# Two single tiles become a pair, and a later pair is projected early, in a fused attention and GLU kernel

## The chip, the cores and the metric

The kernel runs on one core of a Trainium2 chip. The core has a matrix engine (TensorE, PE in the profile; its weight loads are listed as PEld), a vector engine (VectorE, DVE), a scalar engine (ScalarE, ACT), GpSimd (POOL) and SyncE (SP), which here issues the DMAs. The engines run their own instruction streams and wait for one another by semaphores. The metric is the device time of one execution in microseconds; the times shown are medians of several executions.

## The reference

The input `x` has 2048 tokens of 576 values. Two kinds of layers alternate, A B A B, with the same weights both times, each added to its input:

```python
x = x + _A_ref(_layernorm(x), A_wqkv, A_wo)
x = x + _B_ref(_layernorm(x), B_w_gate, B_w_up, B_w_down)
x = x + _A_ref(_layernorm(x), A_wqkv, A_wo)
x = x + _B_ref(_layernorm(x), B_w_gate, B_w_up, B_w_down)
```

A is a local attention with 32 heads of 18 values. It projects the input to q, k and v. A token looks at 8 positions: itself and those 2, 4, ... 14 tokens before it. A softmax over the 8 logits weights the 8 v rows, and the result goes through `wo`. B is a gated unit without a nonlinearity: `(x @ w_gate) * (x @ w_up)` with 4608 columns, then `@ w_down`. Nothing looks further back than 14 tokens, so tokens can be worked on in order, in blocks.

## The kernel before

**Tiles and stages.** 128 tokens are a tile, 16 in all, taken in two groups of eight. A group goes through the first A and B layer, then through the second. A stage is one attention (`attention`, called with its number j) and one GLU (`glu`) for one tile or for a pair of tiles. In the first group's first layer tiles 0, 1, 2 and 3 are stages of their own (j = 0 to 3), tiles 4 and 5 are the pair j = 4, tiles 6 and 7 the pair j = 5. All later stages are pairs; there are 18 stages.

**Forms on TensorE.** A single tile's matmuls use all 128 rows of the array and stream 128 columns (lines 876 and 887 gate and up, 928 and 929 down, 527 the q, k, v projection, 826 the output projection). A pair's matmuls use 64 rows each, two of them side by side, and stream 256 columns (lines 900, 968 and 969, 527, 805). A pair's GLU runs in three phases of six units; a unit is two column blocks of 128 for both gate and up. A single's GLU also has three phases, each of three units of four blocks.

**One attention.** `head` normalizes a tile: statistics on VectorE (lines 414 and 415), the reciprocal root and the scaled copy on ScalarE (429, 430, 439), then the transpose, either on TensorE with a copy by ScalarE (452, 454, 457) when `on_pe` is set, or as a DMA transpose from SP (445). The projection's results are copied out by ScalarE (611, 621, 638, 645). VectorE forms the eight products of q with shifted k (676, 697) and adds them up in part (680 to 685); TensorE sums them to logits with the matrix `Esel` (691); VectorE and ScalarE do the softmax (717 to 731). The probabilities are then spread to all values of a head: with `on_pe` by TensorE with `Bsel` into the bank `pa`, one bank at a time, each copied out by ScalarE (742, 611); otherwise through DRAM by one write and four reads on SP's queue. VectorE multiplies them with shifted v (772) and adds up (786). The output projection follows, and VectorE adds the residual (796). A second `head` prepares the GLU's input. The scratch buffers of products, partial sums and probabilities exist once, so an attention's products wait for the sums of the attention before it.

**PSUM.** The GLU, the projections of q, k and v, and the output projection of pairs share bank pairs (`unit`), three of them at first. The fourth consists of `acct`, which single GLUs use, and `pa`, which the attentions with `on_pe` use; it becomes a unit after the last attention with `on_pe`, j = 4.

**Early work.** Tiles 4 and 5 are loaded into a scratch half of the residual buffer of tiles 2 and 3 (`xtmp`) at the start, and normalized and transposed inside the attention j = 3 (rank 4 there). Their q, k and v have their own place (`q_x`, `kv_x`) in the residual buffers of tiles 4 to 7.

**Order.** Nothing is ordered by hand on the engines. Each step is recorded by `op` with its engine, an assumed cost, what it reads and writes, and a rank. `Plan.run` then places the steps one by one, when the kernel is built, into fixed queues: it takes the step that can start first by the assumed costs, and prefers a lower rank that is ready about then. An attention has its own number as rank, a GLU rank 60, the steps that empty a GLU's banks rank -1. `margin` puts a step later than its inputs are assumed to be ready; `after` binds it to another step.

The pieces that decide the points touched:

```python
        if j == 4:
            return ["x"], q_x, kv_x, 0
        z = (j + 1) % 2
...
        on_pe = j < 5
        prio, mg = (1, 0) if fast else (3, 500 if j < 6 else 1200)
...
                nst = 1 if l == 0 and t < 4 else NST
```

Of the kernel before, what the change touches and what calls it, by code (L numbers as in the profile page):

```python
# [169 lines left out]
def kernel(  # L170
# [12 lines left out]
    nc = tc.nc  # L183
# [222 lines left out]
    def head(src, keys, nst, dst, key, prio, ab, on_pe, mg, c0=0, halves=False):  # L406
# [3 lines left out]
        for i in range(nst):  # L410
            def stats(i=i):
                xr = src(i).rearrange("p (a b) -> p a b", a=2)
                for a in range(2):
                    nc.vector.bn_stats(out=st[:, ia + i, a, :], in_=xr[:, a, :])
# [8 lines left out]
            op("DVE", 970, stats, r=[keys[i]], w=[f"mv{ab}{ia + i}", f"st{ab}{ia + i}0", f"st{ab}{ia + i}1"], prio=prio)  # L423
# [4 lines left out]
        def rs():  # L428
# [3 lines left out]
        op("ACT", 440, rs, r=mk + ["eps"], w=rk, prio=prio)  # L432
        op("DVE", 75, lambda: nc.vector.scalar_tensor_tensor(nmr[:, sl], mv[:, sl, 0], -1.0, rstd[:, sl], op0=ALU.mult, op1=ALU.mult),
           r=mk + rk, w=nk, prio=prio)
        for i in range(nst):
            def apply(i=i):
                x, y = src(i), xn[ia + i]
                sc = dict(bias=nmr[:, ia + i:ia + i + 1], scale=rstd[:, ia + i:ia + i + 1])
                nc.scalar.activation(y[:, 0:D], x, ACT.Identity, **sc)
                if not on_pe:  # L440
                    nc.scalar.activation(y[:, D:D + TL], x[:, KF * P:D], ACT.Identity, **sc)
            op("ACT", 770 if on_pe else 1100, apply, r=[keys[i], nk[i], rk[i]], w=[f"xn{ab}{ia + i}"], prio=prio)
# [41 lines left out]
    def place(j, nst):  # L484
# [3 lines left out]
        if j == 4:  # L488
            return ["x"], q_x, kv_x, 0
        z = (j + 1) % 2  # L490
        return [2 * z, 2 * z + 1], qT_[z][:], kv_[z][:, :, :, 0:HALO + CH], 0

    def attention(j, la, t0, nst):
# [3 lines left out]
        on_pe = j < 5  # L497
        prio, mg = (1, 0) if fast else (3, 500 if j < 6 else 1200)
# [7 lines left out]
        if j != 4:  # L506
            head(lambda i: xin[:, i0 + i, :], xin_k, nst, xnT_A, "xA", prio, 0, on_pe, mg, c0)
# [9 lines left out]
        def project(tag, au, bu, tl, ea, eb, dkeys):  # L517
# [32 lines left out]
            if nst == 2:  # L550
                o = None
                fs = {ka: {}, kb: {}}
                for first in (True, False):
                    for u, key, parts in ((ua, ka, au), (ub, kb, bu)):
                        r0, r1 = (0, 1) if first else (1, 0)
                        kw = dict(pair=(ua, ub), margin=400) if o is None else dict(after=o, need=u)
# [30 lines left out]
            else:  # L587
# [11 lines left out]
                o1 = pieces(ua, au, ka, True, False, late["wo"] if 2 <= j < 4 else None, margin=400, pair=(ua, ub))  # L599
# [44 lines left out]
        else:  # L644
# [12 lines left out]
           r=zk("k0", "k2", "k4", "v0", "v2", "v4"), w=hk, prio=prio)  # L657
        if j == 3:
            pl.rank = 4
            head(lambda i: xtmp[:, i, :], ["xt0", "xt1"], NST, xnT_A, "xA", prio, 0, on_pe, mg)  # L660
            pl.rank = 3
# [72 lines left out]
        op("DVE", 86 + 2.05 * n, soft3, r=["Lt", "zs"], w=["s13"], prio=prio - 1)  # L734
        if on_pe:
# [56 lines left out]
        guard = {3: ["xt0", "xt1"], 5: zk_x}.get(j, [])  # L792
# [40 lines left out]
        head(lambda i: xs_f[:, i0 + i, :], fk, nst, xnT_B[j % NXB], f"xB{j % NXB}_", prio - 1, 1, on_pe, mg, halves=fast)  # L833
# [19 lines left out]
    def glu(j, t0, nst, last):  # L853
# [148 lines left out]
        for ph in range(nph):  # L1002
# [37 lines left out]
            settle(ph, use)  # L1040

    seq = []
    for g0 in range(0, NTT, GT):
        for l in range(n_al):
            t = g0
            while t < g0 + GT:
                nst = 1 if l == 0 and t < 4 else NST
                seq.append((l, t, nst))
                t += nst
# [5 lines left out]
    load_x(2, 1)  # L1055
    load_x(3, 1)
# [6 lines left out]
    for j, (l, t0, nst) in enumerate(seq):  # L1063
        if l == 0 and j >= 4:
# [5 lines left out]
        if j == 4:  # L1070
# [40 lines left out]
```

## Time and profile before

| what | value |
|---|---|
| median of 3 executions | 1057.23 us (1056.66 to 1058.14) |
| the profiled execution, its time | 1056.22 us |
| its span, first to last instruction | 1054.4 us |
| TensorE busy | 1040.7 us, 99% |
| VectorE busy | 786.2 us, 75% |
| ScalarE busy | 410.8 us, 39% |
| mean granted TensorE clock | 0.998 |

The profile is one execution. Its times count from the first instruction of the span. A row of the view by stretches gives the stretch, its length, and for each engine the busy time in it with the number of instructions in brackets; the last three numbers are the granted TensorE clock as a share of full speed, the busy share of the DMA engines, and GB/s. If the view is limited to one engine, only its column stands there, and if limited to one line of the kernel, only that line's instructions are counted. A row of the view in order of time gives start, duration, engine, line, operation, what is written and read, and in brackets the idle time of the engine before it and what ended it. Matmuls overlap their neighbours by some tenths of a microsecond, so the distance from one start to the next says more than a duration.

### The profile page before, as it was taken

The page shows a single profiled execution, that of the slowest core. Times are in us where ns is not written, and L with a number is a line of the kernel's source. Part 1 is how long each engine was busy: PE and PEld are TensorE (multiplying, and loading weights), DVE is VectorE, ACT ScalarE, POOL GpSimd, SP SyncE. Part 2 cuts the span into 40 slices and gives each one's busy share as a digit, 9 for nine tenths or more (in the row PEclk, how much of TensorE's full clock was granted, in tenths as well). Part 3 has the DMA queues.
Part 4 walks back from the last instruction along what each step waited for, and adds up shares of the span by engine and source line. Part 5 has one row for each costly group of instructions (what it writes and reads, how often), then busy time and mean ns, then how long its engine had stood idle before and what let it go on. Part 6 is the DMA issues. An engine that isn't in the chain of part 4 may idle for free.

```text
span 1054.4 us, 39972 instructions
## 1 busy us (share of the span) xinstructions
PE 1040.7 (99%) x17845; PEld 829.9 (79%) x17863; DVE 786.2 (75%) x1477; ACT 410.8 (39%) x1090; POOL 8.9 (1%) x33
## 2 busy tenths in 40 slices
PE   7999999999999999999999999999999999999998
PEld 4888878787788898778887777877887788777776
DVE  7688989786979996979798876676878758833332
ACT  6752254343334544333434323334344252232221
POOL 3000000000000000000000000000000000000000
PEclk9999999999999999999999999999999999999999
DMA  9966563524262543254444534334353334343332
GB/s 272 317 186 194 177 185 104 155 63 145 69 149 81 146 105 107 70 149 128 120 93 107 140 114 118 93 115 95 93 151 82 99 90 126 116 135 96 116 101 69
DMA packets 146828, 133.68 MB, mean 127 GB/s; under 512 B 42272, under 2 KB 146016, under 8 KB 146656
## 3 DMA queue, kind: packets, MB, share of 16 engines
q1 hardware_dynamic: 146656, 131.13, 44.1%
q8 instruction: 139, 2.28, 0.9%
q14 instruction: 33, 0.27, 0.1%
HBM read 118.51 MB, written 4.06 MB: 116 GB/s over the span
## 4 chain that ended last, share of the span: by engine, by line
PE 82%; DVE 11%; DMA 4%; SPq 1%; issue 1%; ACT 1%; DVEq 0%; ACTq 0%
PE pg L900 15%; PE pu L900 14%; PE pu L968 9%; PE pg L968 8%; PE pa L900 5%; PE acct L900 5%; PE pg L527 4%; PE pu L527 3%; PE pu L876 3%; PE pg L876 3%; PE pg L928 2%; DVE scr L772 2%; DVE oT L786 2%; DMA scr<-a_dram 2%; DVE h L912 2%; PE pg L805 1%
## 5 line engine op out<-in xcount | busy, mean ns | idle before, releaser
L900 PE MATMUL pg<-xnT_B,wg 64*128 64x256 bf16 x3072 | 395.3, 269 | 0.5 <-DVE xf L796 0.5
L900 PE MATMUL pu<-xnT_B,wu 64*128 64x256 bf16 x3072 | 395.0, 269 | 0.5
L900 PEld LDWEIGHTS <-wg 64*128 64x128 bf16 x4032 | 367.7, 94 | 29.7 <-issue 2.6
L900 PEld LDWEIGHTS <-wu 64*128 64x128 bf16 x4032 | 366.8, 94 | 23.5 <-issue 0.6
L968 PE MATMUL pg<-wd,h 64*128 64x512 bf16 (+1 forms) x972 | 252.0, 377 | 0.8 <-DVE h L912 0.8
L968 PE MATMUL pu<-wd,h 64*128 64x512 bf16 (+1 forms) x971 | 252.1, 377 | 0.0
L912 DVE TENSOR_TENSOR h<-pu,g_sb 128x512 bf16<-128x512 f32 x228 | 153.5, 686 | 73.8 <-ACT g_sb L911 69.7
L968 PEld LDWEIGHTS <-h 64*128 64x128 bf16 (+1 forms) x1992 | 115.1, 94 | 100.3 <-DVE h L912 2.9
L911 ACT CAST g_sb<-pg 128x512 bf16<-128x512 f32 x228 | 132.1, 586 | 127.6 <-PE pg L900 91.6
L471 ACT COPY tok<-pu 1x1 f32<-1x1 f32 x254 | 37.4, 147 | 258.7 <-PE pu L900 191.8
L900 PE MATMUL acct<-xnT_B,wg 64*128 64x256 bf16 x960 | 130.7, 269 | 0.0
L900 PE MATMUL pa<-xnT_B,wu 64*128 64x256 bf16 x960 | 130.6, 269 | 0.0
L969 PEld LDWEIGHTS <-h 64*128 64x128 bf16 (+1 forms) x1992 | 114.1, 95 | 1.3 <-issue 0.6
L527 PEld LDWEIGHTS <-wqkv 64*128 64x128 bf16 (+1 forms) x2044 | 103.2, 94 | 15.0 <-issue 2.6
L900 PE MATMUL pg<-xnT_B,wgu_t 64*128 64x256 bf16 x384 | 103.3, 269 | 0.0
L900 PE MATMUL pu<-xnT_B,wgu_t 64*128 64x256 bf16 x384 | 103.3, 269 | 0.0
L969 PE MATMUL pa<-wd,h 64*128 64x64 bf16 (+1 forms) x540 | 102.1, 189 | 0.1
L969 PE MATMUL acct<-wd,h 64*128 64x64 bf16 (+1 forms) x540 | 102.1, 189 | 0.0
L697 DVE TENSOR_TENSOR scr<-qT,kv 128x1280 bf16<-128x1280 bf16 x104 | 82.4, 816 | 25.9 <-ACT kv L611 25.9
L786 DVE TENSOR_TENSOR oT<-oT,scr 128x1280 bf16<-128x1280 bf16 (+1 forms) x119 | 90.9, 764 | 3.2
L527 PE MATMUL pg<-xnT_A,wqkv 64*128 64x256 bf16 (+2 forms) x826 | 92.6, 260 | 0.5 <-ACT wqkv L355 0.3
L527 PE MATMUL pu<-xnT_A,wqkv 64*128 64x256 bf16 (+2 forms) x786 | 90.1, 262 | 0.8 <-DVE kv L609 0.4
(156 smaller groups left out, 1598.2 us busy)
## 6 DMA issues: line engine op xcount, KB each, us to landing
wd<-in_B_w_down_dram SPq DMA_DIRECT2D x324, 288.0 KB, 4.4
scr<-a_dram SPq DMA_DIRECT2D x52, 128.0 KB, 2.7
wg<-in_B_w_gate_dram SPq DMA_DIRECT2D x6, 768.0 KB, 10.0
wu<-in_B_w_up_dram SPq DMA_DIRECT2D x6, 768.0 KB, 11.3
out_dram<-xf SPq DMA_DIRECT2D x16, 144.0 KB, 3.0
xb<-in_A_x_dram SPq DMA_DIRECT2D x6, 288.0 KB, 2.9
a_dram<-scr SPq DMA_DIRECT2D x13, 128.0 KB, 2.4
scr<-in_A_wqkv_dram SPq DMA_DIRECT2D x4, 288.0 KB, 3.6
```

What stands on the lines that cost most here:

```text
L471: box["at"] = nc.scalar.copy(tok[0:1, :], src())
L527: return nc.tensor.matmul(bank(p_, u)[0:m, e * n:(e + 1) * n], lhsT=wqkv[r_, k, w0:w0 + m], rhs=xnT_A[r_, k, c0:c0 + n], start=start, stop ...
L697: op("DVE", 70 + 2.6 * n, lambda p_=p_, e=e: nc.vector.tensor_tensor(late["prod"][p_ % 2][:, e, :, 0:n], qT[:, :, 0:n], kT[:, :, HALO - DI ...
L772: nc.vector.tensor_tensor(js(dst), js(vT[:, :, o0:o0 + n]), abw, op=ALU.mult)
L786: op("DVE", 70 + 2.63 * n, lambda i_=i_: nc.vector.tensor_tensor(oT[:, :, 0:n], oT[:, :, 0:n], late["prod"][i_ % 2][:, 0, :, 0:n], op=ALU. ...
L876: nc.tensor.matmul(pt[:, e * n:(e + 1) * n], lhsT=w_[:, k, ft * P:(ft + 1) * P], rhs=xT[:, k, 0:n], start=(first and k == 0 and e == 0), s ...
L900: return nc.tensor.matmul(ps[:, e * n:(e + 1) * n], lhsT=w_, rhs=xT[rows, k, 0:n], start=(first and e == 0 and k == 0), stop=(not first an ...
L911: op("ACT", 490, lambda: nc.scalar.copy(g_sb[gs][:, 0:ul], pg[use["slot"]][:, 0:ul]), r=[f"wg_{j}_{u}"], w=[f"g{gs}"], prio=0, due=True)
L912: op("DVE", 605, lambda: nc.vector.tensor_tensor(hb[hs][:, 0:ul], pu[use["slot"]][:, 0:ul], g_sb[gs][:, 0:ul], op=ALU.mult), r=[f"wu_{j}_{ ...
L928: nc.tensor.matmul((pg, pu)[i][use["slot"]][:], lhsT=lhs, rhs=wt[:, e % 2, 0:512], start=first, stop=fin)
L968: return [lambda: nc.tensor.matmul((pg, pu)[i][use["slot"]][:], lhsT=lhs, rhs=wt[rows, e % 2, 0:512], start=first, stop=fin, skip_group_ch ...
L969: lambda: nc.tensor.matmul((pg, pu)[i][tl["slot"]][:, 0:TL], lhsT=lhs, rhs=wt[rows, e % 2, 512:D], start=first, stop=fin, skip_group_check ...
```

## The change

Tiles 2 and 3 become the pair j = 2, so tiles 4 and 5 are j = 3, tiles 6 and 7 are j = 4, and there are 17 stages. Numbers that name stages move by one or two accordingly: places of q, k and v, the margins, the guards on buffers, and the release of `acct` and `pa`, now after j = 2. `on_pe` holds for j < 3, so the pair of tiles 4 and 5 now spreads its probabilities through DRAM and has its GLU input transposed by DMA; its first `head` runs in attention j = 2, on TensorE.

Tiles 6 and 7 are loaded into `xtmp` once tiles 4 and 5 have been read from it. `head` can be split into its normalizing part (`parts="n"`) and its transposing part (`parts="t"`). For tiles 6 and 7 the first part stands in attention j = 2, behind the step that writes the probabilities (`xr=["s13"]`), the second in attention j = 3. Their projection (j = 4) is bound behind the end of the GLU of stage 1 (`late["glu1"]`). That of tiles 2 and 3 stays bound behind the output projection of tile 0. The second `head` of j = 2 gets priority 0, a margin of 200 and statistics by halves.

```diff
-    def head(src, keys, nst, dst, key, prio, ab, on_pe, mg, c0=0, halves=False):
+    def head(src, keys, nst, dst, key, prio, ab, on_pe, mg, c0=0, halves=False, parts="nt", xr=()):
...
-        if j == 4:
+        if j == 3:
             return ["x"], q_x, kv_x, 0
-        z = (j + 1) % 2
+        z = 1 if j == 2 else j % 2
...
-        on_pe = j < 5
-        prio, mg = (1, 0) if fast else (3, 500 if j < 6 else 1200)
+        on_pe = j < 3
+        prio, mg = (1, 0) if fast else (3, 500 if j < 5 else 1200)
...
-        if j != 4:
+        if j not in (3, 4):
             head(lambda i: xin[:, i0 + i, :], xin_k, nst, xnT_A, "xA", prio, 0, on_pe, mg, c0)
...
-                        kw = dict(pair=(ua, ub), margin=400) if o is None else dict(after=o, need=u)
+                        kw = dict(pair=(ua, ub), margin=400, after=late.get({2: "wo", 4: "glu1"}.get(j))) if o is None else dict(after=o, need=u)
...
-                o1 = pieces(ua, au, ka, True, False, late["wo"] if 2 <= j < 4 else None, margin=400, pair=(ua, ub))
+                o1 = pieces(ua, au, ka, True, False, None, margin=400, pair=(ua, ub))
...
+        if j == 2:
+            pl.rank = 3
+            head(lambda i: xtmp[:, i, :], ["xt0", "xt1"], NST, xnT_A, "xA", prio, 0, on_pe, mg)
+            pl.rank = 4
+            load_x(6, 2, True)
+            pl.rank = 2
         if j == 3:
             pl.rank = 4
-            head(lambda i: xtmp[:, i, :], ["xt0", "xt1"], NST, xnT_A, "xA", prio, 0, on_pe, mg)
+            head(lambda i: xtmp[:, i, :], ["xt0", "xt1"], NST, xnT_A, "xA", prio, 0, False, mg, parts="t")
             pl.rank = 3
...
+        if j == 2:
+            pl.rank = 4
+            head(lambda i: xtmp[:, i, :], ["xt0", "xt1"], NST, xnT_A, "xA", prio, 0, False, mg, parts="n", xr=["s13"])
+            pl.rank = 2
...
-        guard = {3: ["xt0", "xt1"], 5: zk_x}.get(j, [])
+        guard = {2: ["xt0", "xt1"], 4: zk_x}.get(j, [])
...
-        head(lambda i: xs_f[:, i0 + i, :], fk, nst, xnT_B[j % NXB], f"xB{j % NXB}_", prio - 1, 1, on_pe, mg, halves=fast)
+        head(lambda i: xs_f[:, i0 + i, :], fk, nst, xnT_B[j % NXB], f"xB{j % NXB}_", 0 if j == 2 else prio - 1, 1, on_pe, 200 if j == 2 else mg, halves=fast or j == 2)
...
+        late[f"glu{j}"] = chain["pe"]
...
-                nst = 1 if l == 0 and t < 4 else NST
+                nst = 1 if l == 0 and t < 2 else NST
...
-    load_x(2, 1)
-    load_x(3, 1)
+    load_x(2, 2)
     load_x(4, 2, True)
...
-        if l == 0 and j >= 4:
+        if l == 0 and j >= 3:
             load_x(t0, nst)
...
-        if j == 4:
+        if j == 2:
             op("PE", 0, lambda: None, w=list(pool_keys["pa"]) + ["acct"], free="unit", use={"slot": NB})
```

More of the change, by code (lines that the diff above doesn't have):

```diff
@@ L404 @@
     wok = ["wo_z", "wot0", "wot1"] + [f"wo{dd}" for dd in range(4)]
-    def head(src, keys, nst, dst, key, prio, ab, on_pe, mg, c0=0, halves=False):
+    def head(src, keys, nst, dst, key, prio, ab, on_pe, mg, c0=0, halves=False, parts="nt", xr=()):
         mv, st, rstd, nmr, xn = mv_[ab], st_[ab], rstd_[ab], nmr_[ab], xn_[ab]
         ia = c0 // P
-        for i in range(nst):
+        for i in range(nst if "n" in parts else 0):
             def stats(i=i):
@@ L422, in head @@
                 continue
-            op("DVE", 970, stats, r=[keys[i]], w=[f"mv{ab}{ia + i}", f"st{ab}{ia + i}0", f"st{ab}{ia + i}1"], prio=prio)
+            op("DVE", 970, stats, r=[keys[i], *xr], w=[f"mv{ab}{ia + i}", f"st{ab}{ia + i}0", f"st{ab}{ia + i}1"], prio=prio)
         mk = [f"mv{ab}{ia + i}" for i in range(nst)]
@@ L431, in head @@
         rk = [f"rstd{ab}{ia + i}" for i in range(nst)]
-        op("ACT", 440, rs, r=mk + ["eps"], w=rk, prio=prio)
-        op("DVE", 75, lambda: nc.vector.scalar_tensor_tensor(nmr[:, sl], mv[:, sl, 0], -1.0, rstd[:, sl], op0=ALU.mult, op1=ALU.mult),
-           r=mk + rk, w=nk, prio=prio)
+        if "n" in parts:
+            op("ACT", 440, rs, r=mk + ["eps"], w=rk, prio=prio)
+            op("DVE", 75, lambda: nc.vector.scalar_tensor_tensor(nmr[:, sl], mv[:, sl, 0], -1.0, rstd[:, sl], op0=ALU.mult, op1=ALU.mult),
+               r=mk + rk, w=nk, prio=prio)
         for i in range(nst):
@@ L441, in apply @@
                     nc.scalar.activation(y[:, D:D + TL], x[:, KF * P:D], ACT.Identity, **sc)
-            op("ACT", 770 if on_pe else 1100, apply, r=[keys[i], nk[i], rk[i]], w=[f"xn{ab}{ia + i}"], prio=prio)
+            if "n" in parts:
+                op("ACT", 770 if on_pe else 1100, apply, r=[keys[i], nk[i], rk[i]], w=[f"xn{ab}{ia + i}"], prio=prio)
+            if "t" not in parts:
+                continue
             cs = slice(c0 + i * P, c0 + (i + 1) * P)
```

## The prediction

> **What bounds the kernel now.** I read the page's head first, then the chain of work that ended last, then the span cut at the stage borders.
>
> ```profile
> span 1054.4 us, 39972 instructions
> PE 1040.7 (99%) x17845; PEld 829.9 (79%) x17863; DVE 786.2 (75%) x1477; ACT 410.8 (39%) x1090; POOL 8.9 (1%) x33
> PE 82%; DVE 11%; DMA 4%; SPq 1%; issue 1%; ACT 1%; DVEq 0%; ACTq 0%
> ```
>
> ```profile
> 60.00:111.00 51.00, 50.74 (x776) 40.15 (x776) 42.49 (x100) 19.12 (x42) 0.00 (x0) 1.00 0.53 163
> 111.00:188.00 77.00, 76.37 (x1209) 61.62 (x1215) 69.09 (x135) 34.07 (x76) 0.00 (x0) 1.00 0.54 155
> 188.00:400.00 212.00, 210.10 (x3682) 174.41 (x3682) 180.47 (x332) 88.43 (x249) 0.00 (x0) 1.00 0.43 113
> 400.00:1054.00 654.00, 650.23 (x11427) 514.17 (x11423) 450.28 (x806) 229.68 (x645) 0.00 (x0) 1.00 0.39 109
> ```
>
> The columns are length, then busy time of PE, PE's weight loads, DVE, ACT and POOL, then granted clock, DMA share and GB/s. From 60 us on TensorE is idle for 0.26, 0.63, 1.90 and 3.77 us in the four stretches. So whatever shortens its instruction stream shortens the kernel one for one, and whatever makes it wait costs one for one. VectorE is next: 42.49 of 51 and 69.09 of 77 us while the first four GLUs run.
>
> That VectorE share decides how soon an attention is ready. Here are VectorE's stretches from the first score product of one attention to that of the next (single tile 2, single tile 3, pair 4 and 5, pair 6 and 7).
>
> ```profile
> 61.03:87.57 26.54, 22.02 (x52) 1.00 0.49 155
> 87.57:115.36 27.79, 23.70 (x56) 1.00 0.63 192
> 115.36:165.91 50.55, 45.26 (x88) 1.00 0.58 162
> 165.91:215.24 49.33, 41.56 (x75) 1.00 0.48 136
> ```
>
> The attentions follow one another without a gap, since they share the product and probability buffers. Two singles take 54.33 us, a pair 50.55 us.
>
> **The change part by part.** First the TensorE stream. Each row is one step cut out of its stretch (length, PE busy): one single GLU third, one pair GLU third, the projections of tiles 2 and 3, a pair's projection in two pieces, one of the four output projections of tiles 2 and 3, that of a pair, a transpose of tile 2, the two transposes of the pair 4 and 5 ahead of its GLU, the logit sums of tiles 2 and 3 and of a pair, and two of the four probability spreads of the pair 4 and 5.
>
> ```profile
> 131.13:140.65 9.52, 9.47 (x162) 1.00 0.60 189
> 231.68:249.79 18.11, 18.11 (x332) 1.00 0.40 117
> 40.36:44.23 3.87, 3.87 (x73) 1.00 1.08 309
> 44.47:48.26 3.79, 3.79 (x80) 1.00 1.06 343
> 169.38:173.42 4.04, 4.04 (x75) 1.00 0.75 220
> 175.01:178.10 3.09, 3.09 (x56) 1.00 0.60 191
> 87.22:87.83 0.61, 0.61 (x8) 1.00 0.05 13
> 165.74:168.30 2.56, 2.56 (x39) 1.00 0.73 212
> 94.94:95.44 0.50, 0.50 (x10) 1.00 0.75 265
> 173.67:174.40 0.73, 0.57 (x9) 1.00 0.00 0
> 178.10:178.61 0.51, 0.51 (x9) 1.00 0.00 0
> 69.83:70.11 0.28, 0.28 (x19) 1.00 1.09 366
> 98.96:99.19 0.23, 0.23 (x18) 1.00 0.00 0
> 134.68:135.02 0.34, 0.34 (x21) 1.00 1.09 393
> 143.33:143.64 0.31, 0.31 (x5) 1.00 0.51 95
> 145.32:145.54 0.22, 0.22 (x5) 1.00 0.93 168
> ```
>
> The spread's matmuls alone (line 742), those of tiles 2 and 3 and those of the pair:
>
> ```profile
> 70.00:110.00 40.00, 1.54 (x8) 1.00 0.59 182
> 140.00:152.00 12.00, 1.53 (x4) 1.00 0.84 216
> ```
>
> 1. Tiles 2 and 3 as a pair. GLU: both thirds hold a logit sum (0.34), so two single GLUs take 6 x 9.18 = 55.08 us, a pair 3 x 17.77 = 53.31: 1.77 saved. Projection: 7.66 against 7.13: 0.53 saved. Output projection: 4 x 0.61 = 2.44 against 2.56: 0.12 lost. Logit sums: 0.51 against 0.34: 0.17 saved. Spreads: 1.54 busy against 1.53: nothing. Together 2.35.
>
> 2. Tiles 4 and 5 lose their TensorE transposes ahead of the GLU (1.24) and four TensorE spreads (0.31 and 0.22 shown, so 1.06): 2.30 saved. In their place come two DMA transposes, and one write and four reads through DRAM, on SP's queue, with ScalarE losing four copies of some 0.6 us. These lie on the attention's path, not on TensorE's, and their GLU then has the 53 us GLU of the pair 2 and 3 ahead of it: hidden. Without that cover the price is the latency, which barely differs (spread on TensorE 142.97 to 151.59; through DRAM 190.78 to 199.60, rows below).
>
> 3. Mode changes. In the single GLUs the 64-row work of pairs is an interruption; inside a pair GLU it is not. The piece 169.38 holds about 72 matmuls, and at the 0.055 us each that the pair GLU shows (18.11 us for some 332) would take 3.95 instead of 4.04. Several such pieces (pair 6 and 7, later layer of tiles 0 and 1) move to places without a change of form. From 0 (they change places only) to 1.0 (some eight pieces at 0.12); I take 0.5, near the middle, as the two pieces above show 0.1 each.
>
> 4. Tiles 6 and 7: loaded a second time into the scratch half, normalized (two statistics of about 1.0 us on VectorE, two applies on ScalarE, two SP transposes) at the probabilities of tiles 2 and 3, and projected after the second GLU. The same instructions ran before, later; new is one 288 KB input load. Where they fall, VectorE waits for the spread anyway (3.31 us idle in the row at 151.59), ScalarE is busy 19.12 of 51 us and DMA 0.53. On SP they pass weight loads for GLU 1, which have seven buffers. Priced at nothing; if the idle time isn't there, 2 us more of VectorE ahead of the pair's output projection.
>
> 5. The two input loads made one, and the bank for pair GLUs given free after the pair 2 and 3 instead of 4 and 5: nothing, by the same cover.
>
> Sum of the stream: 2.35 + 2.30 + 0.5 = 5.15 us less, from 4.65 to 5.65.
>
> **The wait that it brings.** GLU 1 ends at 111.03 now. Without tile 2's output projection (1.22) and transpose (0.50), with the projection 0.53 and the logit sums 0.17 shorter, it ends at 108.6. GLU 2 then needs both tiles of the pair. These rows (start, duration) give the clock of a pair's attention.
>
> ```profile
> 134.10 0.81 DVE L414 BATCH_NORM_STATS2 st<-xb 128x6 f32<-128x288 bf16 x2
> ...
> 142.29 0.68 DVE L731 TENSOR_TENSOR scr<-scr,zs 128x512 bf16<-128x512 f32 x1
> ...
> 151.59 0.83 DVE L772 TENSOR_TENSOR oT<-xf,scr 128x1280 bf16<-128x1280 bf16 x1 [3.31 <-ACT scr L611]
> ...
> 190.09 0.69 DVE L731 TENSOR_TENSOR scr<-scr,zs 128x512 bf16<-128x512 f32 x1
> ...
> 199.60 0.83 DVE L772 TENSOR_TENSOR oT<-kv,scr 128x1280 bf16<-128x1280 bf16 x1 [1.88 <-DMA scr<-a_dram]
> ```
>
> The pair's attention starts at 61.03, as tile 2's did in its row above. The pair of 50.55 us carried about 3 us that this one will not have ahead of its end: statistics of two tiles (134.10 and the next, 1.9 us; now in the spread's wait) and of later-layer tiles. That gives 47.5, end 108.5. Bounds: its busy time alone, 45.26, ends at 106.3; the whole 50.55 at 111.6. From the start of the output projection of the pair 4 and 5 (165.74) to its first transpose's end (174.40) it is 8.7 us; with the second transpose and copy 10. So GLU 2 can begin at 118 to 119.
>
> TensorE has until then: rest of GLU 1 to 108.6, output projection 2.56, transposes 1.24, projection of tiles 6 and 7 7.13: 119.5. The fill is just as long as the wait. What remains are hand-overs: there are three PSUM bank pairs, the output projection takes two, the projection two, twice; so one waits until the other's banks are read out, once by two residual adds on VectorE and once by two copies on ScalarE. No row shows such a hand-over with nothing else to run; with instructions of half a microsecond (0.81 to 0.83 us is VectorE's longest above) I estimate 0.9 and 0.8, so 1.7 us of idle time. It is 0 if the order in the queue meets it, 6 if the output projection falls behind the first half of the projection (below).
>
> An idle TensorE can lose its clock here as well:
>
> ```profile
> 12.00:14.00 2.00, 0.56 (x25) 0.32 (x26) 1.90 (x4) 2.00 (x4) 0.00 (x0) 1.00 0.97 260
> 16.00:18.00 2.00, 1.67 (x16) 1.12 (x10) 1.46 (x5) 0.67 (x2) 0.00 (x0) 0.50 0.94 294
> ```
>
> After 1.4 us of idle time in two, the granted clock was 0.50 two microseconds later. Some 3 us at half clock would cost 1.5. My 1.7 us come in two pieces of under 1 us, so I add nothing; this is in the upper end. [...]
>
> Gain 5.1 - 1.7 = 3.4 us. The profiled execution took 1056.22 (span 1054.4 and 1.8 around it), so 1052.8 by its own clock; the median 1057.23 lies 1.0 above it, so **1053.8** as a median.
>
> Afterwards nothing should be late: VectorE begins the pair 4 and 5 at about 108 instead of 115, while GLU 2 lasts to some 180 with what is put into it.
>
> **The rivals.** Faster or slower "by over 0.2%" means 2.1 us here, about what a measurement can tell.
>
> A, no change: the wait is filled in the wrong order. TensorE's order is fixed when the kernel is built. If the pair's attention ends at 109 to 112, the projection of 6 and 7 has begun and holds two of three bank pairs until its first half (4.04) is copied out, about 114; then the output projection, GLU 2 begins at 124, idle 124 - 119.5 = 4.5, up to 6. Time 1057.2 - 5.1 + 4.5 to 6, so 1056.6 to 1058.1. For it: attention and GLU 1 both end near 108.5. Against it: the pair 4 and 5, also with a single GLU around it, began its output projection at 165.74, by the time its attention's stretch was over (165.91).
>
> B, slower: VectorE gains nothing by the pair and also gets the statistics of 6 and 7 ahead of its products: 54.33 + 1.9 = 56.2 us, end at 117.3. TensorE finishes GLU 1 and the projection at 115.7, idles 1.6, runs 2.56 of output projection and then has nothing but 1.24 us of transposes in 7.5 us: idle about 7.9, in one long piece that costs the clock too (1.5). Time 1057.2 - 5.1 + 7.9 + 1.5 = 1061.5. It decides from an attention of about 54 us: end at 115.2, GLU 2 at 125.2, idle 5.7 and the clock's 1.5. For it: two singles did take 54.33. Against it: both pairs measured took under 51.
>
> C, faster still: the hand-overs vanish and half of the 1.90 us idle between 188 and 400 goes, as attentions run earlier: 1057.2 - 5.65 - 1 = 1050.6.
>
> **How the numbers follow.** Forecast (1051.5 to 1055) 0.56, C 0.08, A 0.17, B 0.19. Faster by over 0.2% are the forecast and C, and a hundredth from A's near edge: 0.65; within 0.2%: 0.15; slower: 0.20. The range leaves out B and the far end of C: 1050.8 to 1059.3.
>
> **What would show it.** Right: TensorE's busy sum near 1036; the first 64-row GLU at 119 to 122 with the projection of tiles 6 and 7 directly ahead; less than 2.5 us idle between 105 and 125 with the clock at 1.00; the single GLU groups halved. The order would be wrong (A) if the output projection of tiles 2 and 3 comes after the first half of that projection; B if the pair's last product sum on VectorE ends after 115. The sum of the stream would be wrong if PE's busy time falls by under 4 us, or if idle time appears after 188 us that isn't there now.

## The result and the profile after

The changed kernel takes 1052.43 us (median of 6 executions, 1051.84 to 1053.36) against 1057.87 us before (6, 1056.66 to 1058.58). The ratio is 0.9949, with a 95% interval of 0.9940 to 0.9959: 5.4 us faster. The prediction was 1053.8 us, faster. Ratios here and below are formed from all executions of a run, so they can differ by up to 0.0007 from the quotient of the two medians.

The profiled execution of the changed kernel took 1053.36 us, the slowest of its six; that of the kernel before took 1056.22 us, less than any of its other executions. So the two profiles lie only 2.9 us apart. What a profile can explain is that difference, not the one of the medians.

The page's head, after:

```profile
span 1051.4 us, 40011 instructions
PE 1035.9 (99%) x17890; PEld 832.5 (79%) x17901; DVE 782.5 (74%) x1443; ACT 410.2 (39%) x1105; POOL 8.9 (1%) x33
```

TensorE's busy sum fell by 4.8 us, VectorE's by 3.7. TensorE is still the bound. To see where the time went, both traces are cut at two places: the start of the first single GLU, and the first matmul of the GLU of tiles 4 and 5 that has all of the GLU before it behind it. The view by stretches for TensorE alone (length, busy, clock, DMA share, GB/s), before:

```profile
33.60:188.34 154.74, 153.79 (x2444) 1.00 0.63 185
188.34:1054.40 866.06, 859.98 (x15103) 1.00 0.40 110
```

and after:

```profile
33.83:185.88 152.05, 150.33 (x2509) 1.00 0.54 162
181.85:182.94 1.09, 1.09 (x24) 1.00 0.82 253
185.88:1051.40 865.52, 858.58 (x15085) 1.00 0.40 110
```

The middle row after is needed because the two cuts don't hold quite the same work. A pair's GLU ends with down matmuls that the kernel puts behind the first step of the next GLU (`pend` in `glu`). So the first 20 matmuls of the GLU of tiles 4 and 5 already run at 181.85, for 1.09 us, ahead of the last down matmuls of the GLU of tiles 2 and 3 (four of the 24 counted there are still running from before). In the kernel before, the GLU ahead is a single one and nothing runs early. Rows 1 and 3 alone say 2.69 and 0.54 us shorter. With the 1.09 us counted to the second part, the first part is 3.78 us shorter: 4.55 less busy, 0.77 more idle. The second is 0.55 us longer: 0.31 less busy, 0.86 more idle. Apart from the 20, the second parts hold the same number of matmuls of every form. In the first part 14 records of down matmuls are missing before and 7 after, and a matmul without a record counts as idle time, so there the lengths say more than the split. The two parts together are 3.23 us shorter; the load phase ahead of them is 0.23 longer. A second profile of the changed kernel has 152.05 and 865.44 us for rows 1 and 3, with 1.25 us idle in the first in place of 1.72.

All engines by stage up to the GLU of tiles 4 and 5, after (columns as in the prediction's second fence; 121.56 is the first matmul of the first pair GLU, L914):

```profile
60.00:108.00 48.00, 47.74 (x735) 37.89 (x738) 43.83 (x81) 19.57 (x43) 0.00 (x0) 1.00 0.53 163
108.00:121.56 13.56, 12.39 (x188) 9.52 (x187) 13.25 (x29) 6.49 (x18) 0.00 (x0) 1.00 0.51 155
121.56:185.00 63.44, 63.44 (x1136) 51.80 (x1137) 52.00 (x92) 26.50 (x75) 0.00 (x0) 1.00 0.33 95
```

The wait that the change brings is the second row: 1.17 us idle in 13.56. Behind it TensorE runs the first pair GLU, with the pairs' other work inside it, without any idle time.

VectorE in order of time, after: the first score product of the pair of tiles 2 and 3, the end of its softmax, the statistics of tiles 6 and 7, the first product with v, the last sum, and the first product of the next pair.

```profile
61.39 1.55 DVE L707 TENSOR_TENSOR scr<-qT,kv 128x1280 bf16<-128x1280 bf16 x2
...
81.19 0.69 DVE L741 TENSOR_TENSOR scr<-scr,zs 128x512 bf16<-128x512 f32 x1
82.54 0.81 DVE L414 BATCH_NORM_STATS2 st<-xf 128x6 f32<-128x288 bf16 x2
...
90.84 0.82 DVE L786 TENSOR_TENSOR oT<-kv,scr 128x1280 bf16<-128x1280 bf16 x1 [1.73 <-ACT scr L615]
...
106.33 0.82 DVE L800 TENSOR_TENSOR oT<-oT,scr 128x1280 bf16<-128x1280 bf16 x1
...
107.66 1.55 DVE L707 TENSOR_TENSOR scr<-xf 128x1280 bf16<-128x1280 bf16 x2
```

The pair's attention takes 107.66 - 61.39 = 46.27 us and its last sum ends at 107.15. The statistics of tiles 6 and 7 stand in the wait for the spread, of which 1.73 us are left.

TensorE in order of time, after: the output projection of tiles 2 and 3 (L819), the first matmul of the projection of tiles 6 and 7 (L531), the last transposes, and the first pair GLU.

```profile
107.90 0.29 PE L819 MATMUL pg<-wo_p,oT 64*128 64x288 bf16 x1
...
112.27 0.28 PE L531 MATMUL pg<-xnT_A,wqkv 64*128 64x256 bf16 x1
...
119.87 0.40 PE L456 MATMUL pa<-ident,xn 128*128 128x128 bf16 x4
120.19 0.25 PE L458 MATMUL pa<-ident,xn 128*64 128x128 bf16 x2
121.56 0.27 PE L914 MATMUL pg<-xnT_B,wg 64*128 64x256 bf16 x1 [1.12 <-ACT xnT_B L461]
```

The output projection comes before GLU 1 is over, the projection of tiles 6 and 7 fills the chain behind it, and one piece of 1.12 us is left. It ends with ScalarE's copy of the second transpose. ScalarE in order of time, after:

```profile
119.00 0.69 ACT L461 COPY xnT_B<-pa 128x640 bf16<-128x640 bf16 x1
119.59 0.60 ACT L625 ACTIVATE qT<-pg 128x512 bf16<-128x512 f32 x1
120.08 0.59 ACT L615 CAST kv<-pu 128x512 bf16<-128x512 f32 x1
120.54 0.39 ACT L642 ACTIVATE qT<-pg 64x256 bf16<-64x256 f32 x1
120.82 0.69 ACT L461 COPY xnT_B<-pa 128x640 bf16<-128x640 bf16 x1
```

The copy that the GLU needs (120.82) stands behind three copies of the projection. The largest piece of idle time behind the GLU of tiles 4 and 5 is this one:

```profile
301.46 0.27 PE L914 MATMUL pu<-xnT_B,wu 64*128 64x256 bf16 x1 [0.91 <-DVE h L926]
```

In the second profile of the changed kernel it is 0.19 us, and the largest is 1.03 us at 446.4. Before, the largest pieces there are 0.47 and 0.42 us.

### The profile page after: what moved, and what is told of

It reads as the page before. It is cut to its first block, busy times and chain, and to the rows that moved or that the text cites. A ratio compares the mean times of both kernels' runs of the same rounds, so it can differ in the third digit from the quotient of the medians.

```text
span 1051.4 us, 40011 instructions
## 1 busy us (share of the span) xinstructions
PE 1035.9 (99%) x17890; PEld 832.5 (79%) x17901; DVE 782.5 (74%) x1443; ACT 410.2 (39%) x1105; POOL 8.9 (1%) x33
## 4 chain that ended last, share of the span: by engine, by line
PE 83%; DVE 10%; DMA 4%; ACT 1%; SPq 1%; issue 1%; DVEq 0%; ACTq 0%
PE pg L914 17%; PE pu L914 16%; PE pu L982 6%; PE acct L914 6%; PE pa L914 6%; PE pg L982 5%; PE pa L982 5%; PE acct L982 4%; PE pg L531 3%; PE pu L531 3%; DVE scr L786 2%; DVE oT L800 2%; PE pg L819 2%; DMA scr<-a_dram 1%; PE pg L942 1%; PE pu L890 1%
## 5 line engine op out<-in xcount | busy, mean ns | idle before, releaser
L914 PEld LDWEIGHTS <-wg 64*128 64x128 bf16 x4320 | 393.7, 94 | 30.8 <-issue 2.9
L914 PE MATMUL pg<-xnT_B,wg 64*128 64x256 bf16 x3200 | 412.3, 269 | 1.6 <-ACT xnT_B L461 1.1
L914 PEld LDWEIGHTS <-wu 64*128 64x128 bf16 x4320 | 392.4, 94 | 25.3 <-issue 1.7
L914 PE MATMUL pu<-xnT_B,wu 64*128 64x256 bf16 x3200 | 411.3, 269 | 1.0 <-DVE h L926 0.9
L982 PEld LDWEIGHTS <-h 64*128 64x128 bf16 x2136 | 129.1, 94 | 101.0 <-DVE h L926 0.7
L983 PE MATMUL pu<-wd,h 64*128 64x64 bf16 (+1 forms) x1020 | 192.8, 189 | 0.1
L983 PE MATMUL pg<-wd,h 64*128 64x64 bf16 (+1 forms) x1020 | 192.8, 189 | 0.0
L914 PE MATMUL acct<-xnT_B,wg 64*128 64x256 bf16 x1120 | 152.8, 269 | 0.0
L914 PE MATMUL pa<-xnT_B,wu 64*128 64x256 bf16 x1120 | 152.4, 269 | 0.2
L982 PE MATMUL pu<-wd,h 64*128 64x512 bf16 x576 | 149.3, 377 | 0.3 <-ACT tok L475 0.3
L982 PE MATMUL pg<-wd,h 64*128 64x512 bf16 x576 | 149.1, 377 | 0.0
L983 PEld LDWEIGHTS <-h 64*128 64x128 bf16 x2136 | 127.9, 95 | 1.6 <-issue 1.1
L982 PE MATMUL pa<-wd,h 64*128 64x512 bf16 (+1 forms) x491 | 127.0, 377 | 0.0
L982 PE MATMUL acct<-wd,h 64*128 64x512 bf16 (+1 forms) x492 | 126.8, 377 | 0.0
L531 PEld LDWEIGHTS <-wqkv 64*128 64x128 bf16 (+1 forms) x2030 | 103.6, 94 | 14.5 <-issue 2.6
L914 PE MATMUL pg<-xnT_B,wgu_t 64*128 64x256 bf16 x400 | 107.6, 269 | 0.0
L914 PE MATMUL pu<-xnT_B,wgu_t 64*128 64x256 bf16 x400 | 107.6, 269 | 0.0
L531 PE MATMUL pg<-xnT_A,wqkv 64*128 64x256 bf16 (+2 forms) x863 | 100.5, 265 | 0.2 <-ACT wqkv L355 0.2
```

The costliest lines, as they stand in the source:

```text
L531: return nc.tensor.matmul(bank(p_, u)[0:m, e * n:(e + 1) * n], lhsT=wqkv[r_, k, w0:w0 + m], rhs=xnT_A[r_, k, c0:c0 + n], start=start, stop ...
L914: return nc.tensor.matmul(ps[:, e * n:(e + 1) * n], lhsT=w_, rhs=xT[rows, k, 0:n], start=(first and e == 0 and k == 0), stop=(not first an ...
L982: return [lambda: nc.tensor.matmul((pg, pu)[i][use["slot"]][:], lhsT=lhs, rhs=wt[rows, e % 2, 0:512], start=first, stop=fin, skip_group_ch ...
L983: lambda: nc.tensor.matmul((pg, pu)[i][tl["slot"]][:, 0:TL], lhsT=lhs, rhs=wt[rows, e % 2, 512:D], start=first, stop=fin, skip_group_check ...
```

## The experiments

Three questions stood: which part brings the gain; whether the early projection is what makes the pair pay; and how far the result depends on the order in which TensorE's queue was written (rival A) and on when the pair's attention ends (rival B). Ratios are to the kernel before, measured on the same chip. The smaller settings of the change (priority, margin and statistics by halves of the second `head` of j = 2) were not varied.

**The changed kernel again.** It was run once more beside e6, e7 and e8:

> The changed kernel, unchanged, beside the next three on one chip. If the gain of 0.51% by the medians is real, the ratio to the kernel before is 0.994 to 0.996; if the two profiles (3.0 us apart) are nearer to the truth, 0.997.

1053.74 us against 1058.13, ratio 0.9956 (0.9943 to 0.9968): 4.4 us by the medians, 4.7 by the ratio. With the first measurement the change is worth 4.4 to 5.4 us.

**Part 2 alone (e2): tiles 4 and 5 through DRAM in the kernel before.**

```diff
-        on_pe = j < 5
+        on_pe = j < 4
```

> The kernel before with only one part of the change: the pair of tiles 4 and 5 spreads its probabilities through DRAM and has its GLU input transposed by DMA (on_pe for j < 4). If the TensorE stream decides, four spreads and two transposes less save 2.3 us: ratio to the kernel before 0.9978, TensorE busy 1040.7 - 2.5. If the longer route is exposed there, or its ScalarE and SP work delays something, no gain: ratio 1.000 or above.

1057.19 us against 1058.83, ratio 0.9987 (0.9978 to 0.9996): 1.4 us where the work taken away is 2.3, between the two expectations. From the start of the last three single GLU thirds around this pair to the first pair GLU, TensorE in order of time, before:

```profile
140.65 0.33 PE L876 MATMUL pg<-xnT_B,wg 128*128 128x128 bf16 x3
...
188.34 0.28 PE L900 MATMUL pg<-xnT_B,wg 64*128 64x256 bf16 x1
```

and in e2:

```profile
141.34 0.33 PE L876 MATMUL pg<-xnT_B,wg 128*128 128x128 bf16 x3
...
165.71 0.27 PE L527 MATMUL pu<-xnT_A,wqkv 64*128 64x256 bf16 x1 [1.26 <-DVE h L912]
...
189.05 0.28 PE L900 MATMUL pg<-xnT_B,wg 64*128 64x256 bf16 x1
```

It is 47.69 us before and 47.71 in e2, although two transposes and four spreads are gone. 1.26 us of it is a new wait. The rest is spread over the projections, the output projection and the single GLUs, and its cause stays open; the 64-row work lies in seven pieces in both. So by these two traces part 2 alone brings nothing in this stretch, where the pair stands among single GLUs. The reverse, the change with tiles 4 and 5 left on TensorE, does not fit this plan, by its code: the fourth bank pair, which a pair's GLU needs, only exists once no later attention uses the bank `pa`. Part 2 is a condition of part 1, and how much of the gain each brings in the changed kernel stays open.

**Without the early projection (e3): the pair and part 2 alone.** Tiles 6 and 7 are loaded, normalized and projected at their usual place.

```diff
-        if j not in (3, 4):
+        if j != 3:
...
-after=late.get({2: "wo", 4: "glu1"}.get(j))
+after=late.get({2: "wo"}.get(j))
...
-            pl.rank = 4
-            load_x(6, 2, True)
...
-            head(lambda i: xtmp[:, i, :], ["xt0", "xt1"], NST, xnT_A, "xA", prio, 0, False, mg, parts="t")
...
-            head(lambda i: xtmp[:, i, :], ["xt0", "xt1"], NST, xnT_A, "xA", prio, 0, False, mg, parts="n", xr=["s13"])
```

> The changed kernel without the early work on tiles 6 and 7: no second load into the scratch half, no split normalization, no projection bound behind GLU 1. If that projection is what fills the wait, TensorE idles 7 to 9 us ahead of the first pair GLU instead of 1.1, with a loss of clock there of up to 1.5, and the time is 1059 to 1061, so no better than the kernel before. If other work fills the wait anyway, it stays within 1 us of the changed kernel (1052.4).

1060.07 us against 1058.83, ratio 1.0017 (1.0006 to 1.0027). TensorE in order of time between GLU 1 and the first pair GLU, in e3:

```profile
116.18 0.40 PE L456 MATMUL pa<-ident,xn 128*128 128x128 bf16 x4 [2.98 <-ACT xn L440]
116.51 0.31 PE L458 MATMUL pa<-ident,xn 128*64 128x128 bf16 x2
117.60 0.58 PE L456 MATMUL pa<-ident,xn 128*128 128x128 bf16 x4 [0.78 <-ACT xnT_B L461]
118.11 0.32 PE L458 MATMUL pa<-ident,xn 128*64 128x128 bf16 x2
119.22 0.37 PE L904 MATMUL pg<-xnT_B,wg 64*128 64x256 bf16 x1 [0.79 <-ACT xnT_B L461]
```

The chain from output projection to GLU now has nothing beside it: 4.55 us of idle time, and the matmuls of the GLU's start take 0.37 us in place of 0.27, since the granted clock has dropped to 0.50 (from 116.56 to 123.38, last section). The 4.55 us are less than the 7 to 9 that were expected, since this GLU begins 2.3 us earlier than in the changed kernel (119.22 against 121.56); but the 7 us of projection are still to be done behind it. Without the filling the pair is a loss; with it, 0.6 to 0.7% less.

**Without the binding behind GLU 1 (e5).**

```diff
-after=late.get({2: "wo", 4: "glu1"}.get(j))
+after=late.get({2: "wo"}.get(j))
```

> The changed kernel without the binding of the projection of tiles 6 and 7 behind GLU 1; the planner puts it where it is ready, inside GLU 1. If only the amount of TensorE work ahead of the first pair GLU counts, the rest of GLU 1 fills the wait instead and the time stays within 1 us of 1052.4. If the place counts (banks taken from GLU 1 or from the output projection), it is 3 us or more slower.

1055.01 us against 1058.83, ratio 0.9966 (0.9953 to 0.9979), 1.1 to 1.8 us more than the changed kernel's 0.9956 and 0.9949, with intervals that overlap. The projection of tiles 6 and 7 now goes in pieces into GLU 1 (98.87 to 107.51), ahead of the output projection, and yet only 0.16 us of idle time stands ahead of the first pair GLU, at 121.54. From the first single GLU to the end it is 1017.58 us, as in the changed kernel (1051.40 - 33.83 = 1017.57). What the early projection needs is to be out of the way in time, not the place behind GLU 1. The idle time saved, about 1 us, makes the way from the first single GLU to the first pair GLU only 0.41 us shorter (87.32 against 87.73), and behind it 0.41 us are lost again; why was not tested.

**A later attention.** The changed kernel with ten (e4), then with three (e8) more VectorE instructions at the end of the pair's attention; each takes the maximum of a tile with itself and changes no value.

```diff
+        for _ in range(10 if j == 2 else 0):
+            op("DVE", 743, lambda: nc.vector.tensor_tensor(oT[:, :, 0:n], oT[:, :, 0:n], oT[:, :, 0:n], op=ALU.max), r=["oT"], w=["oT"], prio=prio)
```

(`range(3 if j == 2 else 0)` in e8.)

> The changed kernel with ten more VectorE instructions of 0.82 us at the end of the attention of tiles 2 and 3 (the maximum of its sum with itself, which changes no value), known to the planner. If there is no slack left, as the 1.1 us of idle time ahead of the first pair GLU says, TensorE waits 8.2 us longer: 1060.6; and if a long wait loses the clock, 1.5 more: 1062, with a granted clock near 0.5 after it. If the pair's attention had slack, the time grows by under 4 us.

> As with ten more VectorE instructions at the end of the pair's attention, but three (2.5 us). One for one: 2.5 us slower than the changed kernel, with the idle time ahead of the first pair GLU at 3.6 us and the clock still at 1.00, or just lost (then 2 to 3 us more). If there is slack, under 1 us.

Ten: 1065.36 us against 1058.83, ratio 1.0057 (1.0036 to 1.0078), more than was expected: in its trace the first pair GLU begins 7.8 us later than in the changed kernel, and its first 3.6 us run at a granted clock of 0.50. Three: 1058.07 against 1058.13, ratio 1.0003 (0.9991 to 1.0014). So 2.5 us of lateness cost 5.0 us against the changed kernel on the same chip (1.0003 less 0.9956) and eat the whole gain. TensorE in order of time, e8:

```profile
109.86 0.28 PE L531 MATMUL pg<-xnT_A,wqkv 64*128 64x256 bf16 x1
...
113.80 0.28 PE L821 MATMUL pg<-wo_p,oT 64*128 64x288 bf16 x1
...
125.05 0.37 PE L916 MATMUL pg<-xnT_B,wg 64*128 64x256 bf16 x1 [0.79 <-ACT xnT_B L461]
```

and its stretches (TensorE alone):

```profile
120.00:122.00 2.00, 0.11 (x2) 1.00 0.16 55
122.00:124.00 2.00, 0.75 (x10) 1.00 0.00 0
124.00:126.00 2.00, 1.21 (x14) 0.73 0.00 0
126.00:128.00 2.00, 2.00 (x23) 0.50 0.00 0
```

The plan put the first half of the projection of tiles 6 and 7 (L531) ahead of the output projection (L821), which was ready at about 110.5. The first pair GLU begins 3.5 us later than in the changed kernel, and its first 3.3 us (125.05 to 128.34) run at a granted clock of 0.50, worth some 1.6 us: together about the 5.0.

**The statistics of tiles 6 and 7 ahead of the products** (e6), rival B's condition: the normalizing part stands before the attention's products and no longer waits for the probabilities.

```diff
+            head(lambda i: xtmp[:, i, :], ["xt0", "xt1"], NST, xnT_A, "xA", prio, 0, False, mg, parts="n")
...
-            head(lambda i: xtmp[:, i, :], ["xt0", "xt1"], NST, xnT_A, "xA", prio, 0, False, mg, parts="n", xr=["s13"])
```

> The changed kernel with the statistics of tiles 6 and 7 not bound behind the probabilities of tiles 2 and 3 but free to run ahead of their products. If VectorE sets the start of the first pair GLU, the 2 us come on top: 2 us slower than the changed kernel (1054.4 on its scale) and the last sum of the pair's attention 2 us later than 107.1. If VectorE's other waiting time takes them in, no difference within 0.7 us.

1060.03 us against 1058.13, ratio 1.0022 (1.0009 to 1.0035): 7.0 us worse than the changed kernel, not 2. VectorE in order of time, e6:

```profile
94.60 0.83 DVE L783 TENSOR_TENSOR oT<-kv,scr 128x1280 bf16<-128x1280 bf16 x1 [2.94 <-ACT scr L615]
...
110.67 0.82 DVE L797 TENSOR_TENSOR oT<-oT,scr 128x1280 bf16<-128x1280 bf16 x1
```

The first product with v comes 3.76 us later than in the changed kernel (90.84), the last sum 4.34, for two statistics of together 1.9 us: the wait for the spread that they had filled is still there (2.94). VectorE's last step of the softmax even starts 5.26 us later (86.45 against 81.19): one more tile's statistics, two GLU products, a GLU's residual add and 0.8 us of idle time now stand ahead of it too. Again the first half of the projection stands ahead of the output projection (109.56 and 113.50), and the first pair GLU begins at 125.57.

**The order held by a binding.** The projection of tiles 6 and 7 is bound behind the output projection of tiles 2 and 3: in the changed kernel (e9), with the statistics first (e10), and with the three added VectorE instructions (e12).

```diff
-after=late.get({2: "wo", 4: "glu1"}.get(j))
+after=late.get({2: "wo", 4: "wo2"}.get(j))
...
+                    late[f"wo{j}"] = o
```

> The changed kernel with the projection of tiles 6 and 7 bound behind the output projection of tiles 2 and 3 instead of behind GLU 1. In the changed kernel the output projection comes first anyway (107.9 against 112.3), so if its order is already the good one, the time is the same: 0.9945 to 0.996 of the kernel before.

> The kernel with the statistics of tiles 6 and 7 set free (6 us slower than the changed kernel), with the projection of 6 and 7 bound behind the output projection of tiles 2 and 3. If the 6 us came from the order (output projection behind half of the projection, then a wait long enough to lose the clock), only the 2 us of VectorE remain: 1054 to 1055.5, the output projection at 109.5 to 110, the clock at 1.00, ratio 0.996 to 0.9975. If the lateness of the attention itself is what costs, it stays at 1.001 to 1.003.

> The changed kernel with the same three added maximum operations of 2.5 us at the end of the pair's attention as in e8 (each takes the maximum of a tile with itself and changes no value), and with the projection of tiles 6 and 7 bound behind the output projection of tiles 2 and 3, as in e9. Order theory (most of the 5.0 us that e8 lost against the changed kernel comes from half of the projection being put ahead of the output projection, which ends the attention's chain later, and from the half clock behind the idle time that follows): with the order held, only the lateness itself remains, ratio to before 0.997 to 0.999 (1055 to 1057), the output projection starts at about 110.5 directly behind the attention, no slice behind it has a granted clock below 0.95. Lateness theory (the 2.5 us are amplified in whatever order): ratio 0.9995 to 1.001, as e8, with some 4 us of idle time ahead of the first pair GLU.

e9: 1054.84 us against 1058.40, ratio 0.9966 (0.9954 to 0.9977), no better than the changed kernel, whose queue has the output projection first anyway, and just above what was expected. e10: 1057.41 against 1058.40, ratio 0.9991 (0.9979 to 1.0003), 3.3 us better than e6, and between its two expectations. e12: 1054.62 against 1057.80, ratio 0.9967 (0.9951 to 0.9982), 3.8 us better than e8, and slightly better than was expected. TensorE in order of time, e12:

```profile
110.01 0.29 PE L821 MATMUL pg<-wo_p,oT 64*128 64x288 bf16 x1 [0.57 <-DVE oT L803]
...
122.33 0.27 PE L917 MATMUL pg<-xnT_B,wg 64*128 64x256 bf16 x1
```

The attention is 2.5 us longer as in e8, but the output projection follows it at once, the first pair GLU begins 0.8 us later than in the changed kernel in place of 3.5, and its matmuls take 0.27 us. The order and the clock made the larger part of what e8 lost. In e10 the lateness of 4.3 us itself is the larger part: the first pair GLU begins at 124.74, and the clock stays at full speed.

Against e9, which has the same binding, the three instructions of e12 cost nothing that can be measured (0.9967 against 0.9966), and the statistics of e10 some 2.6 us (0.9991). The binding itself may have a price: 0.9966 in e9 against 0.9949 and 0.9956 without it, with intervals that overlap. In e9 the projection lies in three pieces around the transposes in place of two.

**The last copy first.** ScalarE's reciprocal root, scaled copy and copy of the transposes for the first pair GLU get the rank of the steps that empty a GLU's banks, to pass the three copies of the projection; alone (e7) and with the binding of e9 (e11).

```diff
-        head(lambda i: xs_f[:, i0 + i, :], fk, nst, xnT_B[j % NXB], f"xB{j % NXB}_", 0 if j == 2 else prio - 1, 1, on_pe, 200 if j == 2 else mg, halves=fast or j == 2)
+        head(lambda i: xs_f[:, i0 + i, :], fk, nst, xnT_B[j % NXB], f"xB{j % NXB}_", 0 if j == 2 else prio - 1, 1, on_pe, 200 if j == 2 else mg, halves=fast or j == 2, due=j == 2)
```

(Inside `head`, `due` is handed on to these steps.)

> The changed kernel with the normalization and the copy of the transposes of tiles 2 and 3 put ahead of everything else in the plan (rank -1). The 1.1 us of idle time ahead of the first pair GLU end with a ScalarE copy that stands behind three projection copies; if that order is the cause, the idle time falls below 0.4 us and the time by 0.7 us, to 0.9943 of the kernel before where the changed kernel has 0.9949. If the chain before it is the cause, nothing changes.

> Both: the heads of tiles 2 and 3 ahead of everything and the projection of 6 and 7 bound behind the output projection. If the 1.1 us ahead of the first pair GLU are the only idle time left that can be had, 0.5 to 1 us faster than the changed kernel: 0.9945. If the planner gives it back elsewhere, as with the heads alone (1.7 us at 143.8), no gain.

1054.02 us against 1058.13, ratio 0.9954 (0.9941 to 0.9967), and 1053.51 against 1058.40, ratio 0.9954 (0.9934 to 0.9975): no gain. In e7 the idle time ahead of the pair GLU, which begins at 120.42, falls to 0.74 us, not below 0.4 as expected, and a wait appears in the GLU (TensorE in order of time):

```profile
145.03 0.27 PE L531 MATMUL pg<-xnT_A,wqkv 64*128 64x256 bf16 x1 [1.20 <-DVE xf L962]
```

No version was measurably faster than the changed kernel.

## Why the prediction was right, and where its steps were off

**The stream.** 5.15 us less, from 4.65 to 5.65, was predicted; 4.55 + 0.31 = 4.86 is measured, within the bounds. By place: parts 1 and 2 were to bring 2.35 + 2.30 = 4.65 us, nearly all ahead of the GLU of tiles 4 and 5, and 4.55 came there. The 0.5 for mode changes can't be told apart in the 4.55; behind that GLU 0.31 came. The terms of parts 1 and 2 were not tested apart: e2 shows that the 2.30 of part 2 bring nothing in its stretch when the pair stands among single GLUs. In the changed kernel the pair's work lies in the first pair GLU, where the row from 121.56 to 185 has no idle time.

**The wait.** 1.7 us of idle time was predicted as two hand-overs of 0.9 and 0.8 us ahead of the first pair GLU. There is one piece of 1.12 us, behind a row of copies on ScalarE, and 0.05 beside it; against the kernel before, that part of the work has 0.77 us more idle time. The sum of 1.63 us over the whole kernel fits the 1.7 only because 0.86 us lie behind the GLU of tiles 4 and 5, where "afterwards nothing should be late" had put none, and where new idle time was named as a sign of being wrong. It is scattered: 0.91 us in one piece (only 0.19 in the second profile), some small ones, and 0.1 to 0.2 us behind TensorE's last matmul. So by the lengths the way to that GLU gained more than was forecast (3.78 us, against 4.65 - 1.7 = 2.95, or 3.45 with all of the mode changes), and the rest of the kernel lost 0.55 where nothing was to be lost. That the two errors nearly cancel is luck.

**The times on the way.** The attention was put at 47.5 us, between 45.26 and 50.55; it took 46.27 and is ready at 107.15 where 108.5 was expected. GLU 1 was to end at 108.6 without the output projection in it; it ends at 112.27 with 2.55 us of it inside, so it is 1.1 late by that count. The first pair GLU was put at 119 to 122; it begins at 121.56. The order that the forecast assumed held with little to spare: an attention longer by 2.5 us turned it (e8).

**Rival A** was not what happened, but its mechanism is real: in e4, e6 and e8 the output projection stands behind half or all of the projection. Its condition, an attention that ends at 109 to 112, and its outcome, no change, are what e8 shows (1.0003). Its idle time of 4.5 us or more is 2.04 + 1.25 + 0.79 = 4.08 in e8; what was left out is the clock, some 1.6 us on top.

**Rival B** has its condition tested by e6 in part: the statistics ahead of the products cost not 1.9 but 4.3 us, and this was enough for a slower kernel (1.0022), with an attention that ends at 111.5 rather than at the 115.2 that the prediction named as the point of decision. The prediction priced the late attention and the turned order as two cases; in this kernel the first brings the second, and the clock with it. What of the 4.3 us comes from the statistics themselves and what from the other steps that moved ahead of the softmax, no run separates.

**The clock.** The prediction read one early row, 1.4 us of idle time in two, as enough to halve the clock. As a condition that doesn't hold. TensorE alone by stretches, in e10, which had 1.91 us of idle time in one piece (109.99 to 111.90) and kept the clock there:

```profile
110.00:112.00 2.00, 0.10 (x2) 1.00 0.95 296
112.00:114.00 2.00, 2.00 (x34) 1.00 1.00 339
```

Nor does the same program always lose the clock: of the 24 executions of the kernel before that were timed beside e2 to e5, 18 have a mean clock of 1.000 and six of 0.998 or 0.999. One stretch of 3.41 us at half clock makes 0.0016 of that mean. The last section has an estimate of what else may matter. The half clock was put at some 3 us and 1.5 of cost; in e8 it lasted 3.41 us around the first pair GLU, in e3, e4 and e6 6.82, 10.24 and 6.82.

**The median.** The prediction added 1.0 us for the median's distance from the profiled execution. In the runs since, the profiled execution of before lies 1.65 under its median and that of the changed kernel 0.93 over its own. By the profiles' own clock the gain is 2.9 us where 3.4 was predicted; by the medians it is 4.4 to 5.4. The difference of 1.5 to 2.5 us is in the choice of the executions that were profiled, and no profile of these shows where it lies.

## What to carry to other kernels

Before two stages are made one, work out what TensorE has to do while the longer chain runs behind them, and move independent work there: without it this pairing lost 0.2%, with it it won 0.4 to 0.5%. Where such filling shares banks with the chain's own next step, write the order down (here a binding to the output projection); an order that is left to assumed costs turned for 2.5 us and took the whole gain. A saving measured in one place, such as the 2.3 us of transposes and spreads, need not arrive in another: cut the same stretch out of both traces, count that both hold the same matmuls, and compare lengths, not the sums of instructions.

## What the runs showed of the hardware that was not expected

Around the first pair GLU the half clock lasted 3.41 us in e8, and two and three times as long in e3 and e4. Rows of 0.2 us for TensorE alone, around the drop and the return, give both to a few hundredths (a clock of 0.82 over 0.2 us is 0.13 at full and 0.07 at half speed). In e8, which lost the clock twice, the first drop, the second, and the return from it:

```profile
15.60:15.80 0.20, 0.20 (x5) 0.75 1.13 254
...
124.80:125.00 0.20, 0.00 (x0) 0.82 0.00 0
...
128.20:128.40 0.20, 0.20 (x7) 0.65 0.00 0
```

In e3, the same:

```profile
20.80:21.00 0.20, 0.02 (x1) 0.96 1.06 369
...
116.40:116.60 0.20, 0.20 (x6) 0.90 1.02 282
...
123.20:123.40 0.20, 0.20 (x6) 0.54 0.00 0
```

In e4, the drop and the return around that GLU:

```profile
122.60:122.80 0.20, 0.00 (x0) 0.86 0.10 29
...
132.80:133.00 0.20, 0.20 (x6) 0.54 0.00 0
```

From 124.93 to 128.34 it is 3.41 us, from 116.56 to 123.38 6.82, and from 122.74 to 132.98 10.24: one, two and three times 3.41. The two drops of e8 and of e3 lie whole multiples of nearly the same length apart as well: 109.23 us in e8 (15.70 to 124.93) are 32 times 3.413, and 95.58 us in e3 (20.98 to 116.56) are 28 times. In e8 TensorE worked on the GLU nearly from the drop on (125.05), in e3 only from 119.22, in e4 from 129.34. Cut into pieces of 3.41 us from the drop, in these three the clock came back at the end of the first piece that lies wholly, or but for 0.12 us, in the GLU: 124.93 to 128.34 in e8, 119.97 to 123.38 in e3, 129.57 to 132.98 in e4.

What follows is an estimate, from these distances alone: if an execution is divided every 3.413 us, the place of a gap between the borders may matter, and not only its length. In e10 an early drop gives one border:

```profile
15.80:16.00 0.20, 0.20 (x5) 0.80 1.10 219
```

It lies at 15.92. Carried on by 28 times 3.413 us, a border would lie at 111.49, and it would cut the idle piece of 1.91 us (109.99 to 111.90) into 1.50 and 0.41. That this is why e10 kept its clock is argued, not shown by a run. The busy time ahead of a drop does not sort the cases either: e8 kept the clock behind the 3.41 us from 118.10 to 121.51, in which TensorE was busy for 1.75 us, and lost it behind the next 3.41 with 1.13, but the kernel before lost it early, at 14.90, for 3.41 us, behind 3.41 us with 1.89 us of busy time in 72 matmuls.
